# DuoAttention with a skipping mixture of experts: masks on four array tiles, fp16 transposes, earlier small loads, finer routing steps, and all gathers issued early

## The chip, the cores and the metric

The kernel runs on one core of one Trainium2 chip. The metric is the device time of one execution in microseconds (us). Engines are called PE (TensorE; PEld is its weight load), DVE (VectorE), ACT (ScalarE), POOL (GpSimd) and SP (SyncE). Executions of one kernel scatter here by some 2%, and a run that is over 1.5% above the fastest of its kernel is counted as slow and left out of ratios. A trace shows one execution only. PE's clock is given as the share of full speed that was granted: 1.00 is full, 0.50 half.

## The reference, cut to what matters

```python
# attention: 4 batches, 8 heads, 768 positions, head size 64
scores = (q @ k.T) / 8
keep   = causal                               # heads 0, 2, 6
keep   = causal & (key < 4 | in_window_of_64) # the five streaming heads
x      = softmax(where(keep, scores, -1e9)) @ v      # 3072 tokens x 512
# experts: 8, hidden size 1024; a token takes part if x @ w_skip > 0
e      = argmax(x @ w_gate);  g = softmax(x @ w_gate)[e]
out    = x + g * (relu(x @ w1[e]) @ w2[e])    # else out = x
```

## The kernel before

Attention runs batch by batch, one batch's score work beside the output work of the batch before. Every 128-token tile of `x` is written to `out`, transposed on PE and multiplied with the gate weights. When the last tile is gated, a routing chain on DVE and PE makes a table of token numbers (`idg`, `idx`); then, expert by expert, rows are gathered from `out`, go through two matrix products, and are scattered back.

All loads and all gathers and scatters are issued by GpSimd, into one software queue. Weights of experts 0 to 3 have buffers of their own; those of 4 and 5 take over the buffers of q and k, those of 6 and 7 get buffers that are free only when attention is over.

```python
def after_t(b):                    # when batch b is transposed
    if b + 2 < B: load_qk(b + 2)
    if b == 0:    load_w(0)        # both matrices of expert 0
def after_o(b):                    # when batch b's slots are over
    if 1 <= b < 3:
        load_v(b + 1)              # V of batch 2 stands behind expert 0
        load_w(b)
    if b == 2:
        load_w(3)
        load_w(4, qkp, ("qin", "kin"))
...                                # one output tile:
    nc.vector.tensor_tensor(x, avo, rec, op=ALU.mult)   # fp32
    nc.sync.dma_start(out=outr[b, i], in_=xf)
...                                # its transposes: four fp32 matmuls, then
    nc.vector.tensor_copy(xT, ps)                       # fp32 PSUM -> fp16
...                                # expert phase
for e in range(4): gather(e)
load_w(5, qkp, ("qin", "kin"))
for e in (4, 5): gather(e)
...
for e in range(E):
    up_(e + 1); down(e)
    if e == 0: load_w(6, wp2)
    if e == 1:
        for e_ in (6, 7): gather(e_)
        load_w(7, wp2)
```

The softmax here doesn't subtract the row's maximum and nothing guards it: scores larger than these inputs give would overflow.

Of the kernel before, what the change touches and what calls it, by code (L numbers as in the profile page):

```python
# [8 lines left out]
FP32 = mybir.dt.float32  # L9
# [8 lines left out]
B = 4  # L18
# [32 lines left out]
def kernel(  # L51
# [43 lines left out]

    def load_qk(b, split=False):
        q_in[b], k_in[b] = (
            qkp.tile([P, DS * F], FP16, tag=t, name=t)[:, :H * NT * D]
            .rearrange("p (h x) -> p h x", h=H) for t in ("qin", "kin"))
        if split:  # L100
            for x in (slice(0, 3, 2), slice(4, 7, 2), slice(1, 8, 2)):
                nc.gpsimd.dma_start(out=q_in[b][:, x], in_=qr[b, :, x])
                nc.gpsimd.dma_start(out=k_in[b][:, x], in_=kr[b, :, x])
        else:
            nc.gpsimd.dma_start(out=q_in[b], in_=qr[b])  # L105
            nc.gpsimd.dma_start(out=k_in[b], in_=kr[b])  # L106

# [15 lines left out]
    for i in range(2):  # L123
        nc.vector.memset(va[i][:, :, :, D:], 1.0)
    load_qk(0, True)
    load_qk(1)
    load_v(0)

# [28 lines left out]
    band = const.tile([P, P], FP16, name="band")  # L157
    smask = const.tile([P, NT, P], FP16, name="smask")
    up = smask.rearrange("p i c -> p (i c)")
    far = tiny.tile([P, P], FP16, tag="far", name="far", bufs=1)  # L160
# [8 lines left out]
    bmask = const.tile([NR, 4, 2], FP16, name="bmask")  # L169
    bm_i = const.tile([NR, 4], I32, name="bm_i")  # L170

    vsk = const.tile([P, B, 2, 4, V1], FP16, name="vsk")
# [14 lines left out]
    WgAll = const.tile([P, DS, E + 1], FP16, name="WgAll")  # L187

    def consts_1():
        nc.vector.tensor_copy(smask[:D], band[:D].unsqueeze(1).to_broadcast([D, NT, P]))  # L190

        nc.vector.tensor_copy(smask[:N_SINK, 0], tri[:N_SINK, 0])

        nc.vector.memset(up[D:, :D], NEG)
        nc.vector.tensor_copy(up[D:, D:D + 5 * P].rearrange("p (i c) -> p i c", c=P),
                              band[D:].unsqueeze(1).to_broadcast([D, 5, P]))
        nc.vector.tensor_copy(up[D:, D + 5 * P:], band[D:, :D])
        nc.vector.memset(half, 0.0)
        for i in range(2):
            nc.vector.memset(half[i * D:(i + 1) * D, i], 1.0)  # L200
        for t_ in skq:
            nc.vector.memset(t_, 0.0)
        nc.vector.memset(vsk, 0.0)

    def consts_2():
        for i, h in enumerate(SINKS):
            nc.gpsimd.dma_start(
                out=vraw[4 * i:4 * i + 4, :, :D],
                in_=v[:, h, :N_SINK, :].rearrange("b k d -> k b d"))
        nc.gpsimd.iota(bm_i, pattern=[[-4, 4]], base=0, channel_multiplier=1)  # L210
        nc.gpsimd.iota(iota_i, pattern=[[1, P]], base=0, channel_multiplier=0)
        nc.gpsimd.iota(code_i, pattern=[[2 * E, T2], [-1, E]], base=E, channel_multiplier=0)
        nc.gpsimd.iota(tok_i, pattern=[[P, B * NT]], base=0, channel_multiplier=1)
        nc.gpsimd.dma_start(out=WgAll[:, :, :E],
                            in_=moe_w_gate.rearrange("(s p) e -> p s e", p=P))
        nc.gpsimd.dma_start(out=WgAll[:, :, E],
                            in_=moe_w_skip.rearrange("(s p) -> p s", p=P))
        load_v(1)

# [107 lines left out]
    def strm(b, pr, ii):  # L327

        kt, qt = kT[b, pr], qT[b, pr]
        ps = {}  # L330
        for i in ii:
            ps[i] = sp.tile([P, 1024], FP32, tag="s", name="sps")
            for x, y in ((0, 512), (512, S)):
                nc.tensor.matmul(ps[i][:, x:y], ident, up[:, x:y], start=True, stop=False,
                                 skip_group_check=True)
        for n in range(NT):
            c = n * P
            for i in ii:
                nc.tensor.matmul(ps[i][:D, c:c + P], kt[rows[i], c:c + D],
                                 qt[rows[i], c:c + P], start=False, stop=True,  # L340
                                 skip_group_check=True)
            lo, hi = (0 if n == 0 else c + D), min(c + D + P, S)
            for x, y in (((lo, 512), (512, hi)) if lo < 512 < hi else ((lo, hi),)):
                for i in ii:
                    nc.tensor.matmul(ps[i][D:, x:y], kt[rows[i], c + D:c + P],  # L345
                                     qt[rows[i], x:y], start=False, stop=True,
                                     skip_group_check=True)
        for i in ii:
            a = par[b % 2].tile([P, S], FP16, tag="ats", name="ats", bufs=len(SINKS))
            at[b, PAIRS[pr][i]] = a  # L350
            nc.scalar.activation(a, ps[i][:, :S], ACT.Exp, scale=SCALE)  # L351
# [12 lines left out]
    def outp(g, tail=False):  # L364
# [27 lines left out]
        nc.sync.dma_start(out=outr[b, i], in_=xf)  # L392
        xs[g] = xf

    def xt(g, tail=False):
        ps = tp.tile([P, DS, P], FP32, tag="t", name="xps")
        for s in range(DS):
            nc.tensor.matmul(ps[:, s], xs[g][:, s * P:(s + 1) * P], ident32,  # L398
                             is_transpose=True, start=(s == 0), stop=(s == DS - 1))
# [12 lines left out]
    def route(c0, last=False):  # L412
# [51 lines left out]
        for t in range(1, T2 + 1):  # L464
# [5 lines left out]
            ot, code.rearrange("p t e -> p (t e)").unsqueeze(1).to_broadcast([P, n, NSLOT]),  # L470
            wm.unsqueeze(2).to_broadcast([P, n, NSLOT]), op=ALU.is_equal)
        mv = mk("mv", [P, n, NSLOT, 2])
        nc.vector.tensor_tensor(
            mv, ot.unsqueeze(3).to_broadcast([P, n, NSLOT, 2]),
            vals[:, cs].unsqueeze(2).to_broadcast([P, n, NSLOT, 2]), op=ALU.mult)
        ol = mk("ol", [P, n, P])
        nc.vector.tensor_tensor(ol, iota_i.unsqueeze(1).to_broadcast([P, n, P]),
                                lo.unsqueeze(2).to_broadcast([P, n, P]), op=ALU.is_equal)
        yield
        tb = tp.tile([P, NSLOT, 2], FP32, tag="t", name="tbp")  # L480
        for i in range(n):
            nc.tensor.matmul(tb, ol[:, i], mv[:, i], start=(i == 0), stop=(i == n - 1))  # L482
        if last:
# [40 lines left out]
    def after_t(b):  # L524

        if b + 2 < B:
            load_qk(b + 2)
        if b == 0:
# [16 lines left out]
    for b in range(B):  # L545
        for i, steps in enumerate(slots(b)):
# [10 lines left out]
            go_on()  # L557
            if b == 0 and i == 0:
                consts_2()
            if b == 0 and 2 <= i < 5:  # L560
                (consts_3, consts_4, consts_5)[i - 2]()
        after_o(b)

    g0 = (B - 1) * NT
    for i in range(NT + 2):
        if i < NT:
            outp(g0 + i, True)
        if i < NT + 1:
            xt(g0 + i - 1, True)
        gates(g0 + i - 2)  # L570
        if i < NT:
            fills(1)
        if i == 1:
            routing = route(g0 - NT)
        go_on()
    for _ in routing:
        pass
    fills(2)
# [5 lines left out]
    with tc.tile_pool(name="wp2", bufs=E - NW - 2, reuse_waits="tile") as wp2, \  # L584
# [6 lines left out]

        def gather(e):
            for t in range(T2):
                sl = t * E + e
                xg[e, t] = mxp.tile([P, DM], FP32, name=f"xg{e}_{t}")
                nc.gpsimd.indirect_dma_start(  # L596
                    out=xg[e, t], out_offset=None, in_=out[:, :],
                    in_offset=bass.IndirectOffsetOnAxis(ap=idg[:, sl:sl + 1], axis=0),
# [4 lines left out]
        load_w(NW + 1, qkp, ("qin", "kin"))  # L603
        for e in range(4, 6):
            gather(e)


# [4 lines left out]

        hts, xts = {}, {}

        def xin(e):
            xT = m16.tile([P, DS, T2 * P], FP16, tag="xT", name="mxT", bufs=3)
            for t in range(T2):
                ps = mtp.tile([P, DS, P], FP32, tag="mt", name="mtp")
                for s in range(DS):
                    nc.tensor.matmul(ps[:, s], xg[e, t][:, s * P:(s + 1) * P], ident32,  # L620
                                     is_transpose=True, start=(s == 0), stop=(s == DS - 1))
# [25 lines left out]
        def down(e):  # L647
            w2t = wts[e][1]
            for t in range(T2):
# [4 lines left out]
                for f in range(FS):  # L654
                    nc.tensor.matmul(yp, hts[e][:, f, t * P:(t + 1) * P], w2t[:, f],  # L655
                                     start=(f == 0), stop=(f == FS - 1))
                nc.vector.scalar_tensor_tensor(xg[e, t], yp, tab[:, sl, 1:2], xg[e, t],  # L657
                                               ALU.mult, ALU.add)
                sc = nc.gpsimd.indirect_dma_start(  # L659
                    out=out[:, :],  # L660
                    out_offset=bass.IndirectOffsetOnAxis(ap=idx[:, sl:sl + 1], axis=0),
                    in_=xg[e, t], in_offset=None, bounds_check=N - 1, oob_is_err=False)
                tc.declare_no_dep(sc.ins, group="sc", reason="a token has one slot")
# [18 lines left out]
        nc.vector.tensor_copy(cnt_i[:, E:], cmx)  # L682
        for e in range(E):
            if e + 1 < E:
                up_(e + 1)
            down(e)
            if e == 0:
                load_w(NW + 2, wp2)
            if e == 1:
                for e_ in range(6, E):  # L690
                    gather(e_)
                load_w(NW + 3, wp2)

# [99 lines left out]
```

## Time and profile before

| | before |
|---|---|
| median, range | 218.64 us, 216.81 to 219.34 (3 runs) |
| span of the profiled run | 214.1 us |
| PE / DVE busy in it, mean PE clock | 84% / 50%, 0.958 |
| V of batch 2 in the buffers | 74.7 us |
| first gather issued | 129.2 us |
| transposes of expert 0's second tile | 135.2 us |
| start of the last product that is scattered | 204.9 us |

The prediction below shows the slices, stretches, waits and timeline. The chain that ended last, in order of time, runs over a load in the middle of attention; columns are start, duration in us, and what:

```profile
59.83 14.74 DMA va<-in_v_dram
74.66 0.56 DVE vs L273
```

The load of batch 2's V, issued at 59.8, is copied by DVE the moment it lands. And the groups of instructions give what DVE pays for a tile of `x` (columns: busy us and mean ns, then idle time before it):

```profile
L389 DVE TENSOR_TENSOR x<-av,rec 128x512 f32<-128x512 f32 x18 | 12.4, 692 | 0.7
L404 DVE CAST xT<-xps 128x512 f16<-128x512 f32 x17 | 12.0, 707 | 9.9 <-PE xps L398 9.9
```

### The profile page before, as it was taken

What the parts mean: (1) busy time and instruction counts of PE and PEld (TensorE: products, weight loads), DVE (VectorE), ACT (ScalarE), POOL (GpSimd) and SP (SyncE); (2) the same over time, 40 slices, a digit from 0 to 9 for tenths busy, and PEclk for the clock granted to TensorE, in tenths of its full rate; (3) what the DMA queues carried; (4) which work ended last, traced back from release to release, by engine and by line L of the source; (5) the groups of instructions that cost most, each with busy time, mean ns of one, the idle gap of its engine ahead of it and who ended that gap; (6) DMA issues with size and microseconds to landing.
All of it is one profiled execution on the core that took longest, in us unless ns stands there. A gap on an engine that the chain in (4) does not pass through costs nothing.

```text
span 214.1 us, 5390 instructions
## 1 busy us (share of the span) xinstructions
PE 180.6 (84%) x2321; PEld 125.9 (59%) x2321; DVE 107.0 (50%) x258; ACT 85.8 (40%) x120; POOL 73.0 (34%) x84
## 2 busy tenths in 40 slices
PE   6768675899989889898998899799999994899920
PEld 2435343577767768676777653586776772577400
DVE  7703276367777697679777450232433432142420
ACT  2387751677577555774332200243232231123000
POOL 8932283003070007700000007783037007474530
PEclk9999995599999999999999999999999999699995
DMA  5999999999999999999999997789916994899310
GB/s 69 174 203 190 108 64 164 212 238 235 227 246 213 217 229 237 155 246 243 236 243 263 246 228 159 200 198 195 266 55 100 197 194 117 169 188 250 144 64 5
DMA packets 53137, 39.55 MB, mean 185 GB/s; under 512 B 27945, under 2 KB 44329, under 8 KB 53104
## 3 DMA queue, kind: packets, MB, share of 16 engines
q0 software_dynamic: 49648, 32.82, 103.4%
q1 hardware_dynamic: 3456, 6.29, 8.9%
q8 instruction: 20, 0.33, 0.6%
q14 instruction: 13, 0.11, 0.2%
HBM read 56.66 MB, written 10.49 MB: 314 GB/s over the span
## 4 chain that ended last, share of the span: by engine, by line
PE 40%; DMA 26%; issue 16%; POOL 8%; DVE 4%; ACT 3%; POOLq 0%; ACTq 0%; DVEq 0%
DMA va<-in_v_dram 15%; PE myp L655 9%; PE mhp L638 8%; DMA out_dram<-xg,idx 6%; DMA xg<-out_dram,idg 4%; PE sps L267 3%; PE xps L398 3%; PE tbp L482 3%; PE mtp L620 3%; POOL va L111 2%; POOL qin L105 1%; ACT atr L324 1%; POOL kin L106 1%; PE tps L281 1%; PE av L376 1%
## 5 line engine op out<-in xcount | busy, mean ns | idle before, releaser
L324 ACT ACTIVATE atr<-sps 128x1024 f16<-128x1024 f32 (+1 forms) x36 | 31.2, 914 | 13.8 <-PE sps L320 13.5
L596 POOL DMA_INDIRECT xg<-out_dram,idg x16 | 16.3, 1018 | 55.3 <-PE sps L267 39.6
L657 DVE SCALAR_TENSOR_TENSOR xg<-myp,tab,xg 128x512 f32<-128x512 f32 x16 | 12.0, 751 | 26.8 <-PE myp L655 25.8
L659 POOL DMA_INDIRECT out_dram<-xg,idx x16 | 16.1, 1005 | 24.3 <-DVE xg L657 15.5
L267 PE MATMUL sps<-esk,ident 128*128 128x512 f16 x64 | 18.3, 408 | 4.6 <-DVE ident L134 1.8
L655 PE MATMUL myp<-w2t,ht 128*128 128x512 f16 x96 | 22.2, 379 | 0.0
L287 DVE COPY kT<-tps 128x768 f16<-128x768 f16 x16 | 15.2, 950 | 13.6 <-PE tps L281 13.6
L638 PE MATMUL mhp<-mxT,w1t 128*128 128x256 f16 x192 | 21.9, 273 | 0.0
L625 ACT CAST mxT<-mtp 128x512 f16<-128x512 f32 x15 | 8.3, 588 | 32.0 <-PE mtp L620 32.0
L111 POOL DMA_DIRECT2D va<-in_v_dram x8 | 11.6, 1465 | 26.9 <-DVE rec L387 18.9
L638 PEld LDWEIGHTS <-w1t 128*128 128x128 f16 x192 | 18.8, 98 | 3.3 <-issue 0.2
L655 PEld LDWEIGHTS <-ht 128*128 128x128 f16 x128 | 12.9, 101 | 13.1 <-issue 1.4
L642 DVE TENSOR_SCALAR ht<-mhp 128x512 f16<-128x512 f32 x16 | 11.1, 692 | 18.6 <-PE mhp L638 18.6
L644 ACT ACTIVATE ht<-mhp 128x512 f16<-128x512 f32 x16 | 9.6, 597 | 25.9 <-PE mhp L638 15.8
L351 ACT ACTIVATE ats<-sps 128x768 f16<-128x768 f32 x20 | 15.3, 808 | 10.1 <-PE sps L345 10.0
L287 ACT COPY qT<-tps 128x768 f16<-128x768 f16 x16 | 12.8, 798 | 13.4 <-PE tps L281 13.4
L404 DVE CAST xT<-xps 128x512 f16<-128x512 f32 x17 | 12.0, 707 | 9.9 <-PE xps L398 9.9
L398 PE MATMUL xps<-ident,x 128*128 128x128 f32 x96 | 16.2, 293 | 0.2
L620 PE MATMUL mtp<-ident,xg 128*128 128x128 f32 x64 | 9.4, 285 | 6.1 <-DMA xg<-out_dram,idg 5.4
L320 PE MATMUL sps<-qT,kT 64*128 64x512 f16 (+3 forms) x96 | 14.2, 325 | 0.0
L316 PE MATMUL sps<-tri,idl 64*128 64x128 f16 x144 | 11.0, 226 | 3.4 <-ACT atr L324 2.8
L389 DVE TENSOR_TENSOR x<-av,rec 128x512 f32<-128x512 f32 x18 | 12.4, 692 | 0.7
(140 smaller groups left out, 321.4 us busy)
## 6 DMA issues: line engine op xcount, KB each, us to landing
w1t<-in_moe_w_dram POOLq DMA_DIRECT2D x6, 1024.0 KB, 16.9
w2t<-in_moe_w_dram POOLq DMA_DIRECT2D x6, 1024.0 KB, 22.4
out_dram<-x SPq DMA_DIRECT2D x24, 256.0 KB, 6.1
va<-in_v_dram POOLq DMA_DIRECT2D x8, 384.0 KB, 11.4
qin<-in_q_dram POOLq DMA_DIRECT2D x3, 768.0 KB, 10.9
kin<-in_k_dram POOLq DMA_DIRECT2D x3, 768.0 KB, 14.2
qin<-in_moe_w_dram POOLq DMA_DIRECT2D x2, 1024.0 KB, 23.8
kin<-in_moe_w_dram POOLq DMA_DIRECT2D x2, 1024.0 KB, 28.7
```

Source lines behind the costliest of these rows:

```text
L111: nc.gpsimd.dma_start(out=y[:, x, :D], in_=vr[b, :, x])
L267: nc.tensor.matmul(ps[:, :512], ident, fill, start=True, stop=True)
L287: eng(t.rearrange("c (p n) -> c p n", n=NT), ps.rearrange("c n p -> c p n"))
L320: nc.tensor.matmul(ps[i][:, x:x + n], kT[b, pr][rows[i], j * P:(j + 1) * P], qT[b, pr][rows[i], q0:q0 + n], start=False, stop=True, skip_g ...
L324: nc.scalar.activation(at[b, PAIRS[pr][i]][:, o:o + w], ps[i][:, :w], ACT.Exp, scale=SCALE)
L351: nc.scalar.activation(a, ps[i][:, :S], ACT.Exp, scale=SCALE)
L398: nc.tensor.matmul(ps[:, s], xs[g][:, s * P:(s + 1) * P], ident32, is_transpose=True, start=(s == 0), stop=(s == DS - 1))
L596: nc.gpsimd.indirect_dma_start(out=xg[e, t], out_offset=None, in_=out[:, :], in_offset=bass.IndirectOffsetOnAxis(ap=idg[:, sl:sl + 1], axi ...
L620: nc.tensor.matmul(ps[:, s], xg[e, t][:, s * P:(s + 1) * P], ident32, is_transpose=True, start=(s == 0), stop=(s == DS - 1))
L638: nc.tensor.matmul(hp[:, u], w1t[:, s, f * P:(f + 1) * P], xT[:, s], start=(s == 0 and u == 0), stop=(s == DS - 1 and u == 1))
L655: nc.tensor.matmul(yp, hts[e][:, f, t * P:(t + 1) * P], w2t[:, f], start=(f == 0), stop=(f == FS - 1))
L659: sc = nc.gpsimd.indirect_dma_start(out=out[:, :], out_offset=bass.IndirectOffsetOnAxis(ap=idx[:, sl:sl + 1], axis=0), in_=xg[e, t], in_of ...
```

## The change

Its intent (sink rows are the first four keys of a streaming head, fillers are matmuls whose result nobody uses, issued to keep PE busy): mask matmuls of streaming heads on four 64x64 tiles at once; transposes in fp16 from a DVE cast of `x` (18 attention tiles, 6 experts); the sink rows of V and the gate weights loaded right after the first q and k; the routing of the last batch in finer steps with one more batch of filler matmuls, and no filler between its tiles; all gathers issued before the first scatter. The core of the diff:

```diff
-    load_qk(0, True); load_qk(1); load_v(0)
+    load_qk(0, slice(0, 3, 2), slice(4, 7, 2), odd)
+    ... vraw (sink rows of V) ...; load_qk(1, even); load_v(0); more_qk(1, odd)
+    ... WgAll (gate weights) ...; load_v(1)
-            for x, y in ((0, 512), (512, S)):
-                nc.tensor.matmul(ps[i][:, x:y], ident, up[:, x:y], ...)
+        for x, y in ((0, 512), (512, S)):
+            for u in range(2):
+                for i in ii:
+                    nc.tensor.matmul(ps[i][rows[u], x:y], idl[rows[i], 0, :D],
+                                     smask[rows[i], u, x:y], ...)
+        if not tail:
+            xs[g] = xp.tile([P, DM], FP16, tag="x16", name="x16", bufs=2)
+            nc.vector.tensor_copy(xs[g], xf)
@@ tail of attention
-        gates(g0 + i - 2)
-        if i < NT:
-            fills(1)
+        if i != NT + 1:
+            gates(g0 + i - 2)
-        go_on()
+        if i != NT - 1:
+            go_on()
@@ experts
-        for e in range(4, 6):
+        for e in (4, 5):
             gather(e)
+        load_w(NW + 2, wp2)
+        for e in (6, 7):
+            gather(e)
+        load_w(NW + 3, wp2)
+            if e + 2 < E:
+                cast(e + 2)          # fp16 rows for the transposes
             ...
-            if e == 0: load_w(NW + 2, wp2)
-            if e == 1: ... gather(6), gather(7); load_w(NW + 3, wp2)
```

## The prediction

> **What bounds the kernel now.** I first read the slices of the page (5.35 us each): TensorE (PE), its granted clock, the share and the rate of the DMA engines.
>
> ```profile
> PE   6768675899989889898998899799999994899920
> PEclk9999995599999999999999999999999999699995
> DMA  5999999999999999999999997789916994899310
> GB/s 69 174 203 190 108 64 164 212 238 235 227 246 213 217 229 237 155 246 243 236 243 263 246 228 159 200 198 195 266 55 100 197 194 117 169 188 250 144 64 5
> ```
>
> PE is busy in nearly every slice, which tempts one to count matmuls. But from slice 7 to slice 23 (37 to 128 us) the DMA moves 230 GB/s with hardly a dip, so attention runs beside a saturated queue. Twice PE idles and its clock falls (slices 6 and 7, slice 34). Finer stretches, whose last three columns are clock, DMA share and GB/s:
>
> ```profile
> 24.00:26.00 2.00, 0.97 (x6) 0.50 (x6) 0.00 (x0) 1.64 (x3) 0.76 (x1) 1.00 3.41 87
> 26.00:29.50 3.50, 2.82 (x57) 1.70 (x57) 1.28 (x3) 1.39 (x3) 2.13 (x2) 1.00 0.29 1
> 29.50:34.60 5.10, 1.26 (x15) 0.61 (x15) 4.93 (x12) 2.16 (x3) 4.71 (x5) 0.78 2.38 140
> 34.60:43.30 8.70, 7.89 (x92) 5.31 (x91) 3.55 (x7) 3.88 (x4) 0.00 (x0) 0.54 1.51 205
> 58.00:128.00 70.00, 64.36 (x1158) 49.33 (x1157) 50.52 (x140) 35.02 (x49) 12.19 (x12) 1.00 1.38 231
> ```
>
> The DMA stands still from 26 to 29.5 us, in a phase when the queue has everything ahead of it; then PE does 1.26 us of work in 5.1 us and runs at half clock until 43. The view of waits says why:
>
> ```profile
> PE tps L281 <- DVE kT L287: 3.7, 2, 3.1
> DVE vsk L233 <- DMA vraw<-in_v_dram: 4.6, 1, 4.6
> POOL xg L596 <- DMA out_dram<-xg,idx: 11.4, 1, 11.4
> ```
>
> VectorE, in order, waits 4.6 us for the sink rows of V, which were queued behind 3 MB of q, k and v; the K copy behind it holds PE 3.1 us. GpSimd issues every load, and each waits for the DMA eight before it (the order of instructions shows eight semaphores in rotation); with the tiny sink and gate loads late in that rotation, the next V load was not issued until 27.4 us: this is the hole in the DMA.
>
> How full the queue stays shows at the far end, in the K buffers, which later hold w2 of experts 4 and 5:
>
> ```profile
> DMA to landing us min/median/max: 4.3/13.8/43.7
> ```
>
> The 43.7 us is w2 of expert 4: issued at 88.6, landed at 132.3. The first gather, issued at 129.2, feeds PE at 133.0. So compute (end of routing) and DMA (end of the weights) reach the gathers within about 2 us of each other. After that the expert phase is PE-bound except here:
>
> ```profile
> 176.65 1.89 PE L655 MATMUL myp<-kin,ht 128*128 128x512 f16 x8
> 180.52 0.63 PE L620 MATMUL mtp<-ident,xg 128*128 128x128 f32 x4 [1.99 <-DMA xg<-out_dram,idg]
> 182.76 1.09 PE L620 MATMUL mtp<-ident,xg 128*128 128x128 f32 x4 [1.61 <-DMA xg<-out_dram,idg]
> 183.64 3.02 PE L655 MATMUL myp<-kin,ht 128*128 128x512 f16 x8
> ```
>
> The gathers of experts 6 and 7 come after scatters to the same tensor and wait 11.4 us for them (third line of the waits); PE loses 1.99 + 1.61 us, then 1.13 us to a cold clock (3.02 against 1.89): 4.7 us.
>
> **What the Trainium skill says.** "DMA: Bandwidth & Descriptors", SWDGE vs HWDGE vs iDMA: only one software queue is allocated; and Queues, rings and completion order: descriptors are consumed in ring order. So a gather issued early still stands behind weights already queued; the 43.7 us landing agrees. "TensorE: Matmul & The Clock Gate", The HAM clock gate: about 3.4 us of idleness halves the clock; here 3.1 us did (0.54 for 8.7 us). "TensorEngine Tiling (Array Packing)", Tiling Modes: 64x64 gives four independent tiles; the trace shows the score matmuls of two tiles with one start time. "VectorE: DVE Perf Modes", perf-mode tier table: an fp32 copy within SBUF gets 2x, one from PSUM up to 2x in 16 bits, nothing in fp32; before has only the fp32 cast, 0.69 us.
>
> **The change, part by part.**
> Masks: two 128x128 matmul pairs for two heads take 0.75 us (22.54 to 23.29); as waves of four 64x64 tiles I put 0.43. Saves 0.32 x 8 pairs = 2.6 us of PE; single heads gain nothing.
> fp16 transposes in the first 18 tiles: four fp32 ones cost 0.49 us (108.63 to 109.12). The half-width fp16 ones show 12 in 0.36 us, so 0.06 per full one, 0.24 for four: 0.25 x 18 = 4.5 us of PE. VectorE gets a cast (estimate 0.35 from the 2x mode) and loses about 0.28 of each 0.69 copy: no net change.
> Early sink loads: the 3.1 us wait and the half clock go. Batch 1 takes 12.4 us from its first transposes to its third set (30.95 to 43.31), batch 2 takes 6.6 (58.05 to 64.61): 5.8 us.
> So compute could be some 13 us ahead by 107 us. But the V rows of batch 2 landed at 74.6, after 0.9 us of waiting, in a saturated queue. No bytes are removed; the queue gains only its hole. The changed issue order keeps it fed from 3 us on: 3.5 us of standstill less about 0.5 for the tiny loads, so **3.0 us**. Batch 2's V lands near 71.6, while VectorE would want it near 65. Compute falls back to about 3 us ahead there, and gains a further 2.5 in the rest.
> Tail: without the filler, which took one of two PSUM buffers, the output tiles no longer wait for the preceding copy (six periods of about 1.9 us, from 107.9 to 119); I estimate 2.6 us from PE's and VectorE's sums of 9 to 10 us. One step against it: the last routing now has a fourth filler batch before the table matmul. Before, twelve fillers end as VectorE does:
>
> ```profile
> 123.47 2.75 PE L267 MATMUL sps<-esk,ident 128*128 128x512 f16 x12
> 126.17 1.52 PE L482 MATMUL tbp<-mv,ol 128*128 128x32 f32 x12
> 125.17 0.95 DVE L477 TENSOR_TENSOR ol<-iota_i,lo 128x768 f32<-128x768 int32 x1
> ```
>
> Six more at 0.216 us push it back by 1.3 us. Routing then ends at 127.9 - 3.0 - 2.5 - 2.6 + 1.3 = 121.1, and the first gather goes out near 122.4. The weights' data ended near 130.3 (GB/s falls there), now 127.3. Two queued gathers of 256 KB at 350 GB/s (the rate of the backlogged gathers at 152 to 156 us) and 1.6 us of receipt put the second transposes at 130.4 instead of 135.2: **-4.8 us**.
> Expert phase: all gathers early removes the 4.7 us. Six experts in fp16 save 0.88 - 0.48 = 0.40 each: 2.4. The casts (two of 0.35 us in 7.8) fit, VectorE being idle over half of it. PE may start cold, its filler ending 2.7 us before the rows: +0.7 expected. Together **-6.4 us**.
> Sum: -4.8 - 6.4 = -11.2. The end (last scatter, 8 us) is unchanged. 218.2 (mean of the three times) - 11.2 = 207.0.
>
> **Rivals.**
> A: PE is the bound, all its savings count, and loads adapt: 13 us before the tail, 1.3 net in it, 7.1 in experts, so near 197. The PE row speaks for it, 230 GB/s without a dip and the 43.7 us against it.
> B: the DMA hole is not recovered, because the early tiny loads only move the wait in the eight-slot rotation: 210. For it, that every issue still waits for the eighth before; against, that those eight are now short or old.
> C: scatters, now all behind the last weights and gathers, pile up at the end: +3, so 210. Before, a like backlog at 196 to 200 drained at 330 to 419 GB/s, well before the last one.
> D: PE starts the experts cold and VectorE's casts stall behind late gathers: +2 to +3, 209 to 210.
>
> **Range and chances.** Removing the gather stall is nearly certain (4.7 of 218 is 2.2% alone) and the transposes add 2.4; the other half depends on the queue. B and C together give 212; a hole and outputs overlapping better than I think, 203. Faster 0.95, same 0.04, slower 0.01.
>
> **What would show it.** Right: no slice near 64 GB/s before 37 us; no wait of vsk for vraw; clock 1.0 around 35 us; a new VectorE wait of about 6 us for V of batch 2; w2 of expert 4 landing near 129 with PE idle before its first expert transposes; no wait of the gathers for scatters; four mask matmul waves in about 0.43 us; 18 fillers before the last table matmul. Wrong: gathers landing before expert 4's weights (the queue does not order them), or expert transposes at 122 to 126.

## The result, and the profile after

| | before | after |
|---|---|---|
| median, range | 218.21 us, 216.81 to 219.34 (4 runs) | 211.72 us, 209.42 to 212.35 (4 runs) |
| span of the profiled run, mean clock | 214.1 us, 0.958 | 210.6 us, 0.925 |
| V of batch 2 copied | 74.7 | 73.7 |
| first gather issued | 129.2 | 131.5 |
| transposes of expert 0's second tile | 135.2 | 137.7 |
| start of the last scattered product | 204.9 | 201.0 |

The ratio is 0.9686 (95% interval 0.9592 to 0.9781). Ratios here are the mean time of one kernel's fast runs over that of the other's of the same rounds, so not quite the ratio of the medians quoted. The profiled run of after is the slowest of its four and that of before (215.98 us) is faster than its three timed ones, so the two traces show only 3.5 us of a gain of 6.5.

The slices of the changed kernel (5.26 us each):

```profile
PE   6658867999698648898979799788999999999910
PEclk9999999999859978759996999969999999999975
DMA  4999999999999999999999997469999999952010
```

And the stretches that the prediction showed, last three columns again clock, DMA share and GB/s:

```profile
26.00:29.50 3.50, 2.71 (x65) 1.75 (x64) 2.36 (x5) 1.55 (x3) 1.71 (x2) 1.00 2.47 162
29.50:34.60 5.10, 3.25 (x63) 2.10 (x58) 2.44 (x6) 4.06 (x5) 0.88 (x1) 1.00 3.91 142
34.60:43.30 8.70, 8.15 (x158) 6.31 (x158) 5.26 (x12) 7.23 (x10) 0.00 (x0) 1.00 1.28 233
58.00:128.00 70.00, 59.38 (x1060) 46.60 (x1059) 47.87 (x145) 30.48 (x43) 7.74 (x8) 0.87 1.36 225
```

The early fault is mended as meant: no standstill of the DMA, no half clock. But from 58 to 128 us, where before had a clock of 1.00 and PE busy for 64.4 us, after has 0.87 and 59.4 us. The view of waits says what PE waits for:

```profile
DVE vs L274 <- DMA va<-in_v_dram: 4.8, 2, 3.5
PE tps L282 <- DVE xT L413: 4.1, 2, 3.8
PE xps L406 <- DVE x L400: 3.3, 5, 0.9
```

The wait of 4.6 us for the sink rows is gone; a wait of 3.5 us for V of batch 2 is there in its place, with PE waiting 3.8 us behind it. The third line is new: PE waits for the fp16 cast (line 400). The chain confirms both:

```profile
53.25 20.37 DMA va<-in_v_dram
73.72 0.56 DVE vs L274
...
75.92 0.70 DVE x L393
76.64 0.43 DVE x L400
```

V was issued 6.6 us earlier than before and landed 0.9 us earlier. The groups show the price of the cast:

```profile
L400 DVE CAST x<-x 128x512 f16<-128x512 f32 x18 | 9.4, 523 | 0.6
L413 DVE COPY xT<-xps 128x512 f16<-128x512 f16 x17 | 7.2, 421 | 6.4 <-PE xps L406 6.3
```

The copy out of PSUM fell from 707 to 421 ns (12.0 to 7.2 us in all), but the cast adds 9.4: DVE does 4.6 us more in attention. Its longest casts (0.73, 1.05, 0.81, 0.85 us, the median is 0.43) all began while GpSimd was writing descriptors; a fifth that began then, at 86.5 us, took 0.43.

The timeline of PE at the end of routing and the start of the experts, then late in the expert phase:

```profile
124.76 4.04 PE L268 MATMUL sps<-esk,ident 128*128 128x512 f16 x18
128.64 1.42 PE L495 MATMUL tbp<-mv,ol 128*128 128x32 f32 x12
...
137.73 0.66 PE L640 MATMUL mtp<-ident,xg 128*128 128x128 f32 x4 [2.05 <-DMA xg<-out_dram,idg]
...
180.79 0.61 PE L640 MATMUL mtp<-ident,mx 128*128 128x128 f16 x8
181.24 1.89 PE L676 MATMUL myp<-kin,ht 128*128 128x512 f16 x8
182.96 3.66 PE L659 MATMUL mhp<-mxT,w1t 128*128 128x256 f16 x32
```

The 18 fillers hold the table product back to 128.64. The transposes at 180 us, which before had waited 1.99 and 1.61 us, wait for nothing, and an expert takes 7.39 us after another with no gap.

### The profile page after: what moved, and what is told of

Its sections match the earlier page's. It is cut to its first block, busy times and chain, and to the rows that moved or that the text cites.

```text
span 210.6 us, 5486 instructions
## 1 busy us (share of the span) xinstructions
PE 174.3 (83%) x2361; PEld 123.3 (59%) x2361; DVE 114.4 (54%) x293; ACT 86.0 (41%) x120; POOL 73.8 (35%) x86
## 4 chain that ended last, share of the span: by engine, by line
PE 61%; DMA 15%; DVE 7%; ACT 6%; issue 5%; POOL 3%; POOLq 0%; DVEq 0%; ACTq 0%
PE mhp L659 14%; PE myp L676 13%; DMA va<-in_v_dram 10%; PE sps L268 6%; ACT atr L325 4%; PE tps L282 4%; PE sps L321 3%; DMA kin<-in_k_dram 3%; PE xps L406 3%; PE tbp L495 3%; PE sps L317 3%; DMA xg<-out_dram,idg 2%; PE mtp L640 2%; PE sps L337 2%; DVE x L393 2%
## 5 line engine op out<-in xcount | busy, mean ns | idle before, releaser
L659 PE MATMUL mhp<-mxT,w1t 128*128 128x256 f16 x192 | 22.8, 279 | 0.0
L659 PEld LDWEIGHTS <-w1t 128*128 128x128 f16 x192 | 19.3, 100 | 3.9 <-issue 0.6
L268 PE MATMUL sps<-esk,ident 128*128 128x512 f16 x64 | 17.4, 409 | 4.7 <-DVE ident L132 1.8
L676 PEld LDWEIGHTS <-ht 128*128 128x128 f16 x128 | 12.3, 98 | 12.2
L406 PE MATMUL xps<-ident,x 128*128 128x128 f16 (+1 forms) x96 | 12.7, 264 | 4.5 <-DVE x L400 3.3
L268 PEld LDWEIGHTS <-ident 128*128 128x128 f16 x64 | 6.1, 104 | 11.5 <-issue 5.5
L317 PE MATMUL sps<-tri,idl 64*128 64x128 f16 x144 | 10.4, 227 | 2.7 <-ACT atr L325 2.2
L282 PE MATMUL tps<-ident,qin 128*64 128x128 f16 x192 | 9.0, 233 | 4.1 <-DVE xT L413 3.8
L646 ACT COPY mxT<-mtp 128x512 f16<-128x512 f16 x12 | 6.4, 588 | 13.4 <-PE mtp L640 13.4
```

What stands on the lines that cost most here:

```text
L268: nc.tensor.matmul(ps[:, :512], ident, fill, start=True, stop=True)
L282: nc.tensor.matmul(ps[rows[i], n], src[b][:, h, n * D:(n + 1) * D], ident, is_transpose=True, start=(n == 0), stop=(n == NT - 1))
L317: nc.tensor.matmul(ps[i][:, x:x + P], idl[rows[i], u], tri[rows[i], u], start=(u == 0), stop=False, skip_group_check=True)
L406: nc.tensor.matmul(ps[:, s], x[:, s * P:(s + 1) * P], ident if x.dtype == FP16 else ident32, is_transpose=True, start=(s == 0), stop=(s == ...
L659: nc.tensor.matmul(hp[:, u], w1t[:, s, f * P:(f + 1) * P], xT[:, s], start=(s == 0 and u == 0), stop=(s == DS - 1 and u == 1))
L676: nc.tensor.matmul(yp, hts[e][:, f, t * P:(t + 1) * P], w2t[:, f], start=(f == 0), stop=(f == FS - 1))
```

## The experiments

Twelve kernels ran. For each trace I read the same marks: **V**, the start of DVE's copy of batch 2's V; **G**, the issue of the first gather; **X**, the transposes of expert 0's *second* tile (the expectations call this, loosely, the "second expert's transposes"); **S**, the start of the last product that is scattered. "Clock lost" is the sum of 1 minus the granted clock over 1-us windows from 40 to 126 us; it came in lumps of 1.7 us, that is 3.4 us at half clock.

| kernel | cast? | V | G | G - V | clock lost | X | S | S - X | median us | ratio to before |
|---|---|---|---|---|---|---|---|---|---|---|
| before | no | 74.7 | 129.2 | 54.5 | 1.3 | 135.2 | 204.9 | 69.7 | 218.2 | 1 |
| after | yes | 73.7 | 131.5 | 57.8 | 10.2 | 137.7 | 201.0 | 63.2 | 211.7 | 0.969 |
| loads alone | no | 72.4 | 128.4 | 56.0 | 1.7 | 134.2 | 204.0 | 69.9 | 215.0 | 0.988 |
| experts alone | no | 75.0 | 129.5 | 54.5 | 2.0 | 135.1 | 200.5 | 65.4 | 213.1 | 0.983 |
| after, no cast | no | 74.7 | 128.7 | 54.1 | 3.4 | 134.2 | 200.9 | 66.7 | 212.4 | 0.979 |
| after, no 4th filler | yes | 72.5 | 130.1 | 57.6 | 10.2 | 135.8 | 200.9 | 65.2 | 211.8 | 0.975 |
| after, old tail | yes | 72.3 | 128.1 | 55.8 | 5.1 | 134.2 | 199.2 | 65.1 | 212.7 | 0.974 |
| after, V sooner | yes | 68.0 | 127.2 | 59.3 | 5.1 | 133.3 | 198.0 | 64.7 | 208.7 | 0.958 |
| after, expert 4 late | yes | 73.9 | 129.7 | 55.8 | 6.8 | 135.1 | 212.8 | 77.7 | 223.9 | 1.030 |
| mix 1 | no | 68.0 | 120.8 | 52.8 | 0 | 126.5 | 204.2 | 77.7 | 214.5 | 0.988 |
| mix 3 | no | 66.9 | 118.7 | 51.8 | 0 | 126.1 | 196.7 | 70.5 | 210.6 | 0.956 |
| mix 3 + cast | yes | 67.0 | 124.4 | 57.4 | 6.8 | 130.1 | 198.8 | 68.7 | 212.2 | 0.966 |
| mix 4 | no | 67.1 | 121.2 | 54.1 | 1.7 | 131.6 | 196.3 | 64.7 | 207.9 | 0.957 |
| mix 5 | no | 67.6 | 121.2 | 53.5 | 1.7 | 127.0 | 190.4 | 63.5 | 202.1 | 0.922 |

The kernels of the experiments had 6 runs each, before 11 in each set; the medians of before in the three larger sets were 217.7, 216.5 and 217.9 us, and 217.7 in that of mix 5. Before and "experts alone" show only the end of their early half clock, cut off at 40 us. Intervals are half a per cent to one per cent either way, so ratios that differ by less than 0.01 are not told apart. Medians and ranges take in the slow runs, ratios leave them out. All results were correct.

### First set: parts of the change, undone or alone

**The cast of attention undone** (the experts keep theirs). The edit does two things: without the cast, `xt` also goes back to fp32 transposes.

```diff
-        if not tail:
-            xs[g] = xp.tile([P, DM], FP16, tag="x16", name="x16", bufs=2)
-            nc.vector.tensor_copy(xs[g], xf)
```

> The changed kernel with the fp32 transposes of attention put back (no cast of x to fp16 on VectorE before them); everything else as changed. Theory 1, the cast is in the way: its 18 instructions (0.52 us mean, 9.4 us in all, against 5.1 us saved in the copies) stand between the output tile and its transposes and in front of the K copies; PE's gaps of 0.7 to 1.1 us behind it pull the clock to half at 56 to 63 and 86 to 93 us. Then these gaps and half-clock stretches go, routing ends 2 to 4 us earlier and the time falls from 211.7 to about 208 to 210. Theory 2, the load queue decides: V of batch 2 still lands near 73.6 and expert 4's weights near 131, so at most 2 to 3 us can be won whatever compute does: not below 208. Rival, PE time counts: 18 x 0.25 = 4.5 us more PE work, so 213 to 216.

212.36 us (211.09 to 216.55), ratio 0.9787 (0.9725 to 0.9849), so not faster than after: the first theory (208 to 210) missed, the second (not below 208) is not contradicted. In its trace PE reached the V of batch 2 sooner and waited longer:

```profile
74.65 0.56 DVE L274 COPY vs<-va 64x1560 f16<-64x1560 f16 x1 [6.63 <-DMA va<-in_v_dram]
```

Then it was faster (G 2.8 us earlier), and then slower in the expert phase, ending where after ended (S 200.9). So what is won before V is waited away at V, and what is won after it is lost again late. The late loss is two stops of the engines. One lies before the transposes of expert 1's second tile:

```profile
140.76 0.66 PE L637 MATMUL mtp<-ident,xg 128*128 128x128 f32 x4 [2.83 <-ACT mxT L643]
...
182.88 3.65 PE L656 MATMUL mhp<-mxT,w1t 128*128 128x256 f16 x32 [1.08 <-issue]
```

PE waits 2.83 us there, where before and after wait 0.68. The other is 1.08 us before expert 6's first product. Nine of the fourteen traces have the first stop (2.3 to 2.9 us), kernels with and without the change; ten have a second, of 0.3 to 5.9 us, around experts 5 to 7; after has neither. In the first, the view names no releaser for ScalarE's copy, but the trace's semaphore events do: ScalarE waits for PE's signal that the transposes of expert 1's first tile are done. In the nine traces it came 1.6 to 2.2 us after the end that the profile models for these transposes, in the other five 0.02 us after it, and ScalarE started within 0.04 us of it. So this time is lost between PE's matmuls and their signal. I did not find why and come back to the stops below.

**The fourth filler batch taken out.**

```diff
-    for _ in route(g0, True):
-        fills(6)
+    for j, _ in enumerate(route(g0, True)):
+        if j != 2:
+            fills(6)
```

> The changed kernel without the fourth batch of six filler matmuls in the last routing (between the table's indices and its one-hot). If routing's end is what the gathers wait for: 6 x 0.216 = 1.3 us of filler go, the table matmul starts when VectorE is done (1.2 us earlier), and the whole ends 1.2 us earlier, 210.5. If the queue of weights decides (expert 4 landed at 131.0, first gather issued at 131.5), no more than 0.5 us: 211.2.

211.77 us (211.10 to 216.82), ratio 0.9752 (0.97 to 0.9805). DVE's last wait for the table product fell from 2.62 to 1.32 us, so the batch does hold the table back 1.3 us; the time did not move.

**The new order of loads alone**, on the kernel before.

```diff
-    load_qk(0, True)
-    load_qk(1)
-    load_v(0)
+    load_qk(0, slice(0, 3, 2), slice(4, 7, 2), odd)
+    ...vraw...; load_qk(1, even); load_v(0); more_qk(1, odd)
+    ...WgAll...; load_v(1)
```

> The kernel before with only the new order of loads (sink rows and gate weights early, q and k of batch 1 by even and odd heads, V after the even heads). Expected: the 4.6 us wait for the sink rows and the half clock from 33 to 43 us go, 5.8 us in batch 1. Theory 2, the load queue: nearly all of it is given back at V of batch 2, which lands 1 us earlier than before, and at the gathers behind expert 4's weights: 217 (1 us better than 218.2). Rival: the 5.8 us stay: 212.5.

215.04 us (213.32 to 217.90), ratio 0.9884 (0.9816 to 0.9953). The time lies between the 217 expected and the rival's 212.5. V of batch 2 comes 2.3 us earlier than before and DVE waits 2.4 us for it.

**The new expert phase alone**, on the kernel before: all gathers before the loads of experts 6 and 7, and the cast of the gathered rows.

```diff
+        load_w(NW + 2, wp2)
+        for e in (6, 7):
+            gather(e)
+        load_w(NW + 3, wp2)
+            if e + 2 < E:
+                cast(e + 2)
```

> The kernel before with only the expert phase of the change (all gathers ahead of all scatters, weights of the last two experts between them, fp16 casts and transposes from expert 2 on). In the changed kernel this phase, from the second expert transposes to the last scatter-add, took 63.2 us against 69.7: -6.5. If the two phases are independent, as I think, 218.2 - 6.5 = 211.7, so as fast as the whole change, and all the rest of the change is worth nothing. If the phases depend on each other, 213 to 215.

213.11 us (212.00 to 216.68), ratio 0.9831 (0.9765 to 0.9898). The time fits the case that the phases depend on each other (213 to 215). X stayed (135.1), S - X fell from 69.7 to 65.4. These two parts alone give 1.2 and 1.7%, 2.9% together, of the 3.1% of the whole. If the parts add up, which no run tests, masks, attention's transposes and the tail, to which the prediction gave 9.7 us of PE and DVE work (2.6 + 4.5 + 2.6), add nothing that the runs can tell from zero. The masks had no run of their own.

### Second set: which wait holds attention

**Expert 4's weights after the gathers.** If the gathers stand behind those weights in the queue, this frees them.

```diff
-            load_w(4, qkp, ("qin", "kin"))       # at 88 us
@@ after the first eight gathers
+        load_w(NW, qkp, ("qin", "kin"))
         load_w(NW + 1, qkp, ("qin", "kin"))
```

> The changed kernel with one load moved: expert 4's two weight matrices are asked for after the first gathers of the expert phase instead of at 88 us. Theory (the software DMA queue of weights gates the gathers): in the changed kernel expert 4's second matrix lands at 131.0 us and the first gather, issued at 131.5, reaches the transposes only at 137.7; without that load the gathers are issued as soon as the routing table is done (about 128 to 129.5 us) and the second expert's transposes start 2 to 4 us earlier, 134 to 135.5 us; time 208 to 210 us. Rival (the routing chain on VectorE and the gather's own latency set it): the first gather is issued no earlier than 131 us, the transposes stay at 137 us or later, and the time stays at 211 to 212 us.

A plain miss: 223.85 us (222.43 to 227.10), ratio 1.0296 (1.0226 to 1.0367), slower by 3%. The first gather went out only 1.8 us earlier than in after, 129.7 us, as soon as the routing table was done (129.5). So in after, too, it was routing and not the weights that set the gather: there the table was done at 130.9 us and the weights landed at 131.0 us, and I had taken the coincidence for a cause. And the queue now ran dry, which its slices of GB/s show:

```profile
GB/s 66 167 166 154 178 136 213 236 248 226 244 224 202 209 193 148 208 244 231 247 258 194 3 65 193 183 178 211 208 256 194 221 293 208 273 108 52 19 61 4
```

Slices 22 and 23 (122 to 133 us) are nearly empty. The bytes missing there had to be moved later, and the gathers of experts 4 and 5, which were issued behind them, came late; DVE waited for the rows (us in total, times, longest):

```profile
DVE mx L632 <- DMA xg<-out_dram,idg: 9.0, 4, 7.6
```

With stops of 2.9 and 3.9 us, and half clock after the waits for rows (167 to 174 us) and around the second stop (198 to 205), S - X became 77.7.

**Batch 2's V ahead of half of expert 0.**

```diff
         if b == 0:
-            load_w(0)
+            load_w(0, half=0)            # first matrix only
@@ after_o
             load_v(b + 1)
+            if b == 1:
+                load_w(0, half=1)
             load_w(b)
```

> The changed kernel with the second weight matrix of expert 0 loaded after batch 2's V instead of before it. Theory (batch 2's V is late because weights stand ahead of it in the one queue): V of batch 2 lands 2 to 4 us before the 73.6 us of the changed kernel, VectorE's wait for it of 3.5 us and TensorE's of 3.8 us at 75.8 us shrink below 1 us, and the half clock at 76 to 80 us is gone. If expert 4's weights then still gate the first gather, the total moves by less than 2 us (210 to 212 us), since what is won at batch 2 is waited away at the gather; the rival, that the attention phase itself sets the start of the expert phase, gives 207 to 209 us and a first gather 3 us earlier than 131.5.

208.68 us (206.86 to 210.92), ratio 0.9584 (0.9515 to 0.9653). V came at 68.0 us, 5.7 earlier, and the wait was gone:

```profile
67.97 0.56 DVE L278 COPY vs<-va 64x1560 f16<-64x1560 f16 x1 [0.49 <-DMA va<-in_v_dram]
```

G came 4.3 us earlier, as the rival had said. The ratio is 1.0% below after's, just at the limit of what the runs tell apart. Moving half of one expert's weights did at least as much as can be seen of masks, transposes and tail together. But from V to G it took 59.3 us in this trace, longer than any other.

**The old tail.**

```diff
+        gates(g0 + i - 2)
+        if i < NT:
+            fills(1)                     # a filler per tile again
...
+        go_on()                          # at every step again
```

> The changed kernel with the old order in the routing tail: one filler batch per tile, gates of each step as before, the rest of the routing after every step. Theory (the new tail is worth almost nothing: 13.6 us from the first product with V of the last slot to the last gates, against 14.0 before, because without fillers the clock is halved at 110 to 114 us): the time is within 1 us of the changed kernel, 211 to 213 us, and the clock at 110 to 114 us is whole. Rival (what the prediction said, the tail is worth 2.6 us): 214 us, unless the queue hides it.

212.70 us (209.88 to 219.75), ratio 0.9736 (0.9649 to 0.9823), within 1 us of after, as expected. The clock from 82 to 126 us was whole, while after lost it at 111 to 114. Between the tail's start and G the four traces with the old tail lost no clock, and seven of the ten with the new one lost 1.7 or 3.4 us; so the fillers that the change removed seem to have kept the clock up. The three that did without them all lacked the cast.

**Mix 1**: no cast in attention, no fourth filler, V sooner, expert 4 late (the diffs above).

> A candidate that should beat both kernels: the changed kernel without the fp16 cast of attention's x, without the fourth filler batch, with expert 0's second matrix after batch 2's V and expert 4's weights after the first gathers. Theory (the queue gates twice, at batch 2's V and at the first gather, and the cast halves the clock): the first gather issued at 124 to 127 us, second expert's transposes at 130 to 132.5 us, expert phase 63 to 66 us, time 204 to 207 us. Rival (TensorE's own work and its clock set the attention phase): gather at 128 us or later as in the run without the cast, time 209 to 212 us.

214.54 us (212.97 to 221.32), ratio 0.9878 (0.9811 to 0.9944). Attention did better than I had expected, gathers at 120.8 us in place of 131.5 and no lost clock, and all of it was paid back: S - X is 77.7 us. Again the queue stood empty (45 GB/s in the slice from 118 to 123 us), and again DVE waited for rows of expert 4 (7.4 us, until 158.2). A late stop is there too:

```profile
190.91 6.36 PE L663 MATMUL mhp<-mxT,w1t 128*128 128x256 f16 x32 [3.66 <-ACT mxT L650]
```

6.36 us where 3.66 is usual is the half clock after that stop.

### Third set: the queue and the cast together

**Mix 3**: mix 1 with only expert 4's *second* matrix late.

```diff
-            load_w(4, qkp, ("qin", "kin"))
+            load_w(4, qkp, ("qin", "kin"), half=0)
@@ after the first eight gathers
+        load_w(NW, half=1)
```

> The candidate of the last batch mended: no fp16 cast of attention's x, no fourth filler batch, expert 0's second matrix after batch 2's V, and now only expert 4's SECOND matrix after the first gathers, its first one still at about 88 us. Theory (two gates: batch 2's V, copied at 68.0 us in that candidate against 73.7 in the changed kernel, and a DMA queue that must not stand idle before the gathers, as it did for about 7 us there): first gather issued at 120.5 to 123 us, second expert's transposes at 126 to 129, expert phase 64 to 67 us in place of about 76, time 201 to 205 us. Rival (any weight taken from the time before the gathers must be paid in full after them): expert phase 70 us or more, time 208 us or more.

210.64 us (206.72 to 219.73; three of six runs counted slow), ratio 0.9556 (0.9456 to 0.9656). G 118.7 and X 126.1 were as early as hoped, or earlier. In numbers the rival came true all the same (S - X of 70 us or more, 208 us or more): PE stood for 5.86 us before expert 7's first product (the next expectations call it, wrongly, expert 6's, and put it down to its weights):

```profile
184.77 4.97 PE L664 MATMUL mhp<-mxT,w1t 128*128 128x256 f16 x32 [5.86 <-issue]
```

The trace speaks against the weights. They were asked for at 154.8 us, and where landings of these loads are recorded, in after and in mix 5, they took 17 to 20 us. ScalarE fits better: it stood 7.25 and 1.53 us before its two copies of expert 7's transposes, which ended at 184.71, just before PE went on. It waited, as in the stops above, for a signal of PE: the transposes end at 177.2 us as modelled, and the signal that released the second copy came at 184.11. Why so late is not known.

**Mix 4**: both matrices of expert 4 early, as in after.

```diff
-            load_w(4, qkp, ("qin", "kin"), half=0)
+            load_w(4, qkp, ("qin", "kin"))
```

> As the run before, but with both of expert 4's matrices early, as in the changed kernel. Theory (the gathers stand behind the weights in one queue): the first gather is issued at 121 to 123 us, when the routing table is done, but lands only after the weights, so the second expert's transposes start at 128 to 131 us; expert phase 63 to 66; time 203 to 207 us. Rival (the queue does not delay the gathers): transposes at 126.5 to 127.5 us as with the weights late, time 201 to 204.

207.93 us (206.78 to 211.17), ratio 0.9568 (0.9496 to 0.9640). X came at 131.6, a little past the 128 to 131 expected, far from the rival's 127. Here the first gathers do stand behind weights. Issued at 121.2 us, they reached PE 8.6 us later (4.5 us in mix 5 below):

```profile
129.80 1.11 PE L644 MATMUL mtp<-ident,xg 128*128 128x128 f32 x4 [5.03 <-DMA xg<-out_dram,idg]
```

**Mix 3 with the cast back in.** The pair tells the cast's effect where V is not the gate.

```diff
+        if not tail:
+            xs[g] = xp.tile([P, DM], FP16, tag="x16", name="x16", bufs=2)
+            nc.vector.tensor_copy(xs[g], xf)
```

> As the first run of this batch, but with the fp16 cast of attention's x on VectorE and its fp16 transposes. Theory (the cast's VectorE time makes PE gaps that halve the clock): from the copy of batch 2's V to the first gather 56 to 58.5 us, against about 53 without the cast, with half-clock stretches after 75 us; time 3 to 5 us longer than without the cast. Rival (the half clock came from the wait for batch 2's V and the cast is harmless, its fp16 transposes save 2 us of PE after that): time equal to or up to 2 us shorter than without the cast.

212.15 us (209.45 to 215.65), ratio 0.9661 (0.9571 to 0.9752). In the traces V to G took 57.4 us with the cast and 51.8 without. The two rows of the clock, first with and then without the cast:

```profile
PEclk9999999999999995599999699999999999987995
```

```profile
PEclk9999999999999999999999996999999999978995
```

The times agree in direction: the three fast runs without the cast took 206.7 to 209.0 us, the three with it 209.5 to 210.9, 2.2 us more on average. But the intervals of the ratios overlap, so the size of 3 to 5 us that I had expected is not shown in time; the late stop, 5.9 us without the cast and 2.5 with it, hides a part.

### Fourth set: a version that beats both

**Mix 5**: mix 3 with the late matrix asked for after the gathers of experts 0 and 1, before those of 2 and 3.

```diff
-        for e in range(4):
+        for e in range(2):
             gather(e)
         load_w(NW, half=1)
+        for e in (2, 3):
+            gather(e)
```

> The candidate with expert 4's second matrix late, but asked for after the gathers of experts 0 and 1 alone, ahead of those of experts 2 and 3 (GpSimd spends 1.3 us on each gather, so it enters the queue some 5 us sooner). What is known: with it after eight gathers the gathers landed early (first transposes that wait: 124.8 us) but TensorE later waited 5.9 us for expert 6's first matrix; with it before all gathers the transposes waited until 129.8 us but no long wait came later. Theory (the queue must carry the same bytes and only its idle or slow time is lost; that candidate's rate fell to 120 to 160 GB/s at 130 to 133 us): transposes at 124 to 126 us, the later wait shrinks to 1 to 4 us, time 204 to 207 us, at or below both candidates. Rival (the bytes decide and their order no longer matters): 207 to 209 us like both.

202.06 us (200.45 to 206.09), ratio 0.9215 (0.9148 to 0.9283): 7.8% below before, and better than I had expected. X came at 127.0, and of the long late stop nothing is left:

```profile
172.45 3.66 PE L666 MATMUL mhp<-mxT,w1t 128*128 128x256 f16 x32
179.84 3.66 PE L666 MATMUL mhp<-mxT,w1t 128*128 128x256 f16 x32
```

These are experts 6 and 7, 7.39 us apart, 10.5 us earlier than in after. Moving one weight matrix each of experts 0 and 4, and taking two parts of the change out again, gained a further 4.9% on after (0.9215 over 0.9686), more than the change itself had. The time agrees with the theory, its mechanism is only half shown: the rows do come as early as in mix 3 (X 127.0 and 126.1) and the stop is gone, but since the stop was not a wait for weights as far as the trace tells, why it went is open.

## Why the prediction was right or wrong

The verdict and the range were right (211.72 us, at the upper end of 203 to 212), and 207.0 was 4.7 us too low. The upper end had been reckoned from rivals B and C; C did not occur, and what filled the range is lost clock, which no rival named, so that it held is in part luck. Step by step, by the traces:

**"Expert phase: all gathers early removes the 4.7 us", in all -6.4.** Right. S - X fell from 69.7 to 63.2, 6.5 us, with no gather waiting for a scatter. The cold start was dearer than the 0.7 us allowed for (from X to the transposes of expert 1's second tile it took 1.6 us more than before), other terms cheaper. But after was free of the late stops; the other kernels with the same order of gathers and of expert 4's weights had 64.7 to 66.7 us, so that it came within 0.1 us is luck.

**"Six more at 0.216 us push it back by 1.3 us."** Right as a wait (2.62 against 1.32 us), without effect on the time.

**"Batch 2's V lands near 71.6", from a hole of 3.0 us.** The mechanism was right, the size off: V was copied at 73.7 in the profiled run, 0.9 us earlier than before; the five other kernels with the same loads ahead of V had 72.3 to 74.7, so 0 to 2.4 us. The hole is gone, but over the first 20 us the rate fell from 159 to 135 GB/s, while from 20 to 53 us it rose from 169 to 199: by 53 us some 0.5 MB more had moved (33 x 30 less 20 x 24, in KB), about 2.2 us at the 230 GB/s of the following stretch, and not 3.0.

**"VectorE would want it near 65".** DVE wanted it at 70.2 (73.7 less its wait of 3.5), because PE ran at half clock from 56 to 63 us, after two waits of 0.7 and 0.9 us for casts of 1.05 and 0.81 us. Without the cast DVE was there at 68.0; what took it from 65 to 68 was not looked into. As V was late anyway, this cost nothing then.

**Compute "gains a further 2.5 in the rest", the cast means "no net change", and the tail: "I estimate 2.6 us".** This is the step that failed, the dearest of all. From V to G I had 50.8 us (122.4 less 71.6), before took 54.5, and after took 57.8. PE's own work shrank as forecast or better: the eight mask matmuls of a pair take 0.35 us at full clock (forecast 0.43), four fp16 transposes 0.23 (forecast 0.24). The 7.0 us too few lie in other terms of the sum:

- The cast. Estimated at 0.35 us, it took 0.43 at best and 0.52 on average, and it is in front of PE's transposes, so PE waits for it. Net DVE work is +4.6 us, not 0. Worse is the clock: the trace loses 3.4 us of clock at 87 to 94, which starts after a PE wait of 1.06 us for DVE at 85.2 (a K copy held up behind a cast of 0.85 us and the routing). V to G was 51.8 to 54.1 us in the five kernels after the change that lack the cast and 55.8 to 59.3 in the six that have it. The pair of mix 3, which differs in the cast alone, differs by 5.6 us, in one trace each; its exact share in after is not shown. Nor is it shown that DVE's cast is what does it: the cast brings the shorter transposes with it (0.23 us for four in place of 0.49), and no run tells PE's waits for the cast from PE's having less to do.
- The wait for V. 3.8 us of PE idle put the clock at half from 77 to 80, 1.7 us lost. I had counted the wait and forgotten the clock after it.
- The tail. From the first reciprocal of the tail (108.8 us) to the last gates (122.4) after took 13.6 us, before 14.0. The filler's buffer was no longer in the way, but without fillers the clock fell at 111 to 114, 1.7 us lost, and with the old tail it did not.

The clock lost between V and G in after is 6.8 us, about the whole miss. If it is taken off (an estimate, as clock lost need not all be time lost), 51.0 us are left in after, where 50.8 were forecast, 50.1 to 51.6 in four of the other five kernels with the cast (54.1 in the fifth, V sooner), 51.3 to 52.8 in the five without it, and 54.5 in before. So the sum failed where it took the clock for granted; that DVE had more to do hardly shows beyond that.

What the Trainium skill says in "TensorE: Matmul & The Clock Gate", The HAM clock gate, namely windows of about 3.4 us, fits the lumps: every loss in these traces is a multiple of 1.7 us, but for the last one of each, which the trace's end cuts off. That idleness of about 3.4 us triggers it does not fit: in after no PE wait from 76 to 126 us exceeds 1.2 us, yet the clock fell twice. Nor did the 3.1 us that the prediction names: in before PE's wait began at 31.5 us, and the clock fell at 32.3. Two waits of 0.3 to 1.1 us went before each of the two falls in after, but such stretches also passed without one: PE was busy for 2.86 of the 3.4 us before the fall at 110.9, and in the kernel without the cast for 2.11 of 3.4 us, up to 117.8, with no fall. So the trigger stays open.

**"The second transposes at 130.4 instead of 135.2", behind the queued weights.** In after they came at 137.7 and nothing was queued in front: routing was late, and the weights were just through. The rule of the one queue was right, as mix 4 shows, but it did not bind here. My check "w2 of expert 4 landing near 129 with PE idle before its first expert transposes" came out nearly as said (131.0 us, 2.05 us idle), for another reason: a check that two causes pass alike is no check. Three readings behind the 130.4 were loose as well: in before the packets of the queued weights ended at 132.0 us, not near 130.3; the gathers' 350 GB/s is the best microsecond, the mean from 152 to 156 us being 280; and the first rows landed 0.35 us after their last packet, where 1.6 us was allowed. Worked out anew from these, the sum gives 131.2, so they nearly cancel.

The miss in X is thus 2.1 (V) + 7.0 (V to G) - 1.8 (G to X was 6.2 and not 8.0) = 7.3 us: 137.7 in place of 130.4. By the traces the whole gain is 3.5 us, by the medians 6.5; the difference is which executions were traced.

**What I did not see at all.** Three kernels that reached G 1.4 to 3.4 us earlier than after (no cast, no fourth filler, old tail) ended S within 1.7 us of it and were no faster in time: they lost it in the stops of the expert phase (3.0 to 4.0 us of PE gaps after X in their traces, where after has 0.7 and mix 5 has 2.2). What the stops are stays open, but for the late signals of PE; that they go with the kernel, and not with the single execution, is suggested by mix 3 and mix 5, whose fast runs lie at 206.7 to 209.0 and 200.5 to 202.7 us. Rival B (hole not recovered) and D (cold start, casts stall) each held a part of the truth; rival A (PE is the bound) is refuted, rival C (scatters pile up) did not occur: the scatters began at 177.4 us and were through in time.

## What to carry to other kernels

When one DMA queue is busy nearly all the time, list the transfers that compute waits for, in order, and ask of each saving where the next one stands: here V of batch 2, then the gathers, and a saving before a gate shows only if that gate moves too. Moving a transfer was worth more here than making instructions cheaper, but a queue that runs dry once pays the lost bytes back later. And an extra DVE step in front of PE is to be judged by the waits it puts between matmuls and the clock lost with it (5.1 to 10.2 us here in the kernels with the cast, 0 to 3.4 in those of the change without it), not by its busy time alone.

## What the Trainium skill lacked or had wrong

- "TensorE: Matmul & The Clock Gate", The HAM clock gate: it ties the half clock to about 3.4 us of idleness. Here two PE waits of 0.48 and 1.06 us, within 4 us, were followed by 6.8 us at half clock (after, 87 to 94 us: 3.4 us of clock lost). The same page does say further down, of one kernel, that frequent short idle times between groups of matmuls made the clock go back and forth, but not how long or how many it takes. And a kernel with fillers in its tail kept a clock of 1.00 where the one without fell to 0.50 at 111 to 114 us.
- "VectorE: DVE Perf Modes", perf-mode tier table: from its 2x I estimated 0.35 us for an fp32 to fp16 copy of 128x512 within SBUF. The traces show 0.43 us as a rule and 0.73 to 1.05 us in four of 18 cases, all of which began while GpSimd was issuing DMAs. The table is not wrong: it has times for 2048 elements, and my estimate left out the fixed time of each instruction, which the same page gives under The TRN2 errata. Nor is the second point lacking: "SBUF — State Buffer", Who interferes with whom, says that DVE's copies in the modes that use two ports and GpSimd block each other.
- "DMA: Bandwidth & Descriptors", Queues, rings and completion order: the page says this of the rings of the hardware queues; here it is borne out for GpSimd's queue as well (in mix 4 a gather issued at 121.2 us reached PE at 129.8, behind the weights). The page lacks a word on what the order costs in a kernel: the loads of expert 4 held the first rows back by about 4 us when issued before the gathers (8.6 us from issue to PE in mix 4, 4.5 in mix 5) and left DVE waiting up to 7.6 us for later rows when issued between them (expert 4 late).
- No page that I read explains the stops of 0.3 to 5.9 us around experts 1 and 5 to 7 (eleven of fourteen traces), nor the late signals of PE in them: at expert 1's first tile 1.6 to 2.2 us after the modelled end of its matmuls in nine traces, 0.02 us in the other five.
